# One forgetting-attention and gated-FFN kernel: gates loaded once and first, one decay product in half batch 0, first constants as tasks, a new order

## The chip, the core and the metric

The kernel runs on one core of a Trainium2 chip. A core has a matrix engine (TensorE, PE in the views, with its weight loads as PEld), a vector engine (VectorE, DVE), an activation engine (ScalarE, ACT), a general engine (GpSimd, POOL) and a queue engine that here only issues DMA (SyncE, SP). Each works through its own instructions in the order in which they were written, and waits for the others by semaphores. The metric is the time of one execution on the chip in microseconds.

## The reference

Eight batches of eight heads, 576 positions, head width 64. Attention with a decay that sums the logarithms of gates along the sequence, then a feed-forward stage 1024 wide with a short convolution as its gate. `attn_out` is the product of `attn` with V, and `hp` is `h` with one row of zeros at each end.

```python
scores = scale * np.matmul(q, k.transpose(0, 1, 3, 2))
log_f = np.log(np.clip(f, 0.0001, 1.0))
cum = np.cumsum(log_f, axis=-1)
decay = cum[:, :, :, None] - cum[:, :, None, :]
scores = np.where(causal, -1000000000.0, scores + decay)
scores = scores - np.max(scores, axis=-1, keepdims=True)
attn = np.exp(scores)
attn = attn / (np.sum(attn, axis=-1, keepdims=True) + 1e-09)
...
x = np.ascontiguousarray(attn_out.transpose(0, 2, 1, 3)).reshape(B, S, H * D)
...
h = np.maximum(x @ w_in, 0.0)
...
for k in range(K):
    conv_out += conv_w[k][None, None, :] * hp[:, k:k + S, :]
gate = 1.0 / (1.0 + np.exp(-conv_out))
return (h * gate @ w_out).astype(np.float32)
```

## The kernel before, in words

**Tiles.** The work is cut into 16 half batches of four heads (`hb` 0 to 15) for attention and 8 batches (`b`) for the feed-forward stage. A half batch holds two pairs of heads. For each pair PE makes the diagonal blocks of the score matrix (task `sd`) and, for each head, the blocks right of the diagonal (`so`); the last 64 positions of the four heads are one more task (`st`). ACT exponentiates them (`ed`, `eo`, `et`, lines 355, 372 and 334). PE multiplies by V (`pv`, lines 391 and 396), DVE normalises (`n`, `m`, lines 405 and 407), PE turns the result over (`t`, line 416), and DVE or ACT copies it (`tx`, line 419). Then for each of eight slices of the 1024 wide layer: PE `f` (line 431), ACT relu `r` (442), DVE convolution `c` and `d` (448, 450), ACT tanh or sigmoid `a` (453), DVE gate `g` (460, 458). PE makes the output from all eight slices, `o` (line 476); `e` copies it out of PSUM and `s` stores it.

**PSUM.** It is cut into four buffers of two banks, `ps`. Every PE task takes one and the task that reads it gives it back, so at most four results stand unread.

**Q, K and the decay.** Half batches 0 and 1 load Q and K plainly (`ld`), PE transposes them in nine pieces (`tp`, line 166), and ACT or DVE copies each block out of PSUM while it shifts the bits (`cl`, lines 172 and 174). From half batch 2 on, a transposing DMA brings them in (`q`, line 180), and up to 7 DVE clamps them in place (`cl`, line 186). The positions of Q and K use only every other row; rows in between carry the decay, so that one product gives scores and decay at once. They come from an image in DRAM, which the kernel writes (`ki`, line 281, three DMAs, from the tile `kc`) and reads back for each half batch (`rw`, lines 204 and 205, two DMAs). Half batch 0 doesn't wait for that: with `PAIRS = 2` all its four heads add the decay by two more matmuls after the score matmul (lines 317 and 319), one with `kc` as the stationary operand, one with the selection `sel_q`.

**The decay chain.** The gates `f` are loaded twice, into the upper and lower 64 partitions of one tile (lines 224 and 225, ACT's queue). `dca` clips (DVE, 534), `dcl` takes the logarithm (ACT, 268) and loads the table for exp (269), `dcs` sums (DVE, 272), `dck` makes `kc` (275, 276): the rounded values in partitions 0 to 63 and what rounding left, the low part, in 64 to 127. The constants (`ident`, `mask`, selections) and the first fills are written ahead of all tasks.

**The order.** No scheduler runs. `ORDER`, a string of task names, is written out by hand of a planner; `Plan.play` calls the tasks in that order, and each engine gets its instructions in that order. A name with `@` says which engine takes a task that several can do. `va` casts V (its large part `.0`, its small part `.1`), `wic` and `woc` cast the weights.

Of the kernel before, what the change touches and what calls it, by code (L numbers as in the profile page):

```python
# [700 lines left out]
```

## Time and profile before

| what | us |
|---|---|
| three timed runs | 245.17, 246.23, 246.70 |
| median | 246.23 |
| span of the profiled execution, first to last instruction | 244.7 |
| PE busy in the span | 228.6 |
| DVE busy | 205.5 |
| ACT busy | 206.8 |
| POOL busy | 51.9 |

The profiled execution's own time beyond its span is not recorded; its span lies 1.5 us below the median of the timed runs. A row of a timeline or of the chain begins with its start and its length in us; L166 is line 166; `x9` says how many instructions were put together. What stands in square brackets is idle time of the engine ahead of the row, and who ended it. ACTq and SPq are those engines' sequencers issuing DMAs. The lengths of matmuls overlap, since matmuls are pipelined, so the step from one start to the next is what one costs.

### The profile page before, as it was taken

To read this page: it belongs to the slowest core of one execution; us is meant where nothing else is said; L and a number is where in the kernel's file an instruction comes from. 1 tells how busy PE (TensorE), PEld (TensorE's weight loads), DVE (VectorE), ACT (ScalarE), POOL (GpSimd) and SP (SyncE) were. 2 spreads that over 40 slices of the span, in tenths; PEclk is the share of its full clock that TensorE was granted. 3 is DMA by queue.
4 is the path that set the end of the run, shared out by engine and by line. 5 is a ranking of instruction groups with operands and counts; after the bars stand their busy time and mean duration, and the time that the engine had idled before them with its cause. 6 is when DMAs were issued, how large, how long until landed. Compare 5 with 4: busy or idle time off the path is not lost.

```text
span 244.7 us, 6393 instructions
## 1 busy us (share of the span) xinstructions
PE 228.6 (93%) x2627; PEld 146.1 (60%) x2627; DVE 205.5 (84%) x324; ACT 206.8 (85%) x278; POOL 51.9 (21%) x77
## 2 busy tenths in 40 slices
...
GB/s 189 334 169 250 278 184 189 223 198 306 196 216 196 169 182 220 238 268 251 224 212 274 194 198 269 270 102 196 265 198 227 195 209 4 106 173 77 171 85 216
DMA packets 120424, 49.68 MB, mean 203 GB/s; under 512 B 109879, under 2 KB 110647, under 8 KB 120395
## 3 DMA queue, kind: packets, MB, share of 16 engines
...
q10 hardware_dynamic: 322, 0.47, 0.6%
q8 instruction: 20, 0.33, 0.6%
...
HBM read 21.11 MB, written 10.17 MB: 128 GB/s over the span
## 4 chain that ended last, share of the span: by engine, by line
PE 81%; DMA 5%; DVE 5%; ACT 5%; issue 1%; SPq 1%; ACTq 0%; DVEq 0%
PE ps L476 26%; PE ps L431 23%; PE ps L314 15%; PE ps L391 7%; DMA qk<-image 3%; PE ps L322 3%; PE ps L396 3%; DMA u<-in_f_dram 2%; PE ps L416 2%; ACT qk L172 2%; DVE u L450 2%; DVE u L448 1%; ACT ht L442 1%; ACT pp L372 1%; PE ps L317 1%
## 5 line engine op out<-in xcount | busy, mean ns | idle before, releaser
L431 PE MATMUL ps<-xt,w_in_f 128*128 128x512 f16 (+1 forms) x512 | 71.0, 288 | 0.4 <-DVE xt L419 0.4
L372 ACT ACTIVATE pp<-ps 128x1024 f16<-128x1024 f32 x64 | 64.8, 1032 | 3.7 <-PE ps L314 2.3
L476 PE MATMUL ps<-w_out_f,hg 128*128 128x512 f16 x288 | 66.8, 379 | 0.0
L314 PE MATMUL ps<-qk 128*128 128x128 bf16 (+2 forms) x576 | 63.9, 241 | 2.1 <-DMA qk<-image 0.9
L448 DVE SCALAR_TENSOR_TENSOR u<-ht,cwt 128x576 f32<-128x576 f16 x64 | 52.4, 832 | 4.4 <-ACT ht L442 4.2
L450 DVE SCALAR_TENSOR_TENSOR u<-ht,cwt,u 128x576 f32<-128x576 f16 x64 | 53.9, 856 | 0.5
L453 ACT ACTIVATE hg<-u,cw 128x576 f16<-128x576 f32 x64 | 48.7, 782 | 6.1 <-DVE u L450 6.0
L431 PEld LDWEIGHTS <-w_in_f 128*128 128x128 f16 x512 | 34.7, 99 | 29.4 <-issue 1.3
L314 PEld LDWEIGHTS <-qk 128*128 128x128 bf16 x576 | 39.4, 98 | 19.2 <-issue 2.5
L442 ACT ACTIVATE ht<-ps 128x576 f16<-128x576 f32 x64 | 41.0, 664 | 6.4 <-PE ps L431 2.8
L476 PEld LDWEIGHTS <-hg 128*128 128x128 f16 x288 | 26.9, 98 | 28.9
L460 DVE SCALAR_TENSOR_TENSOR hg<-hg,ht 128x576 f16<-128x576 f16 x51 | 38.6, 767 | 0.6 <-ACT hg L453 0.5
L358 POOL TENSOR_SCALAR_AFFINE_SELECT pp<-pd 128x1024 f16<-128x1024 f32 x16 | 19.7, 1244 | 53.6 <-ACT pd L355 53.6
L391 PE MATMUL ps<-va,pp 128*128 128x65 f16 x640 | 25.3, 194 | 1.7 <-DVE va L219 1.7
L391 PEld LDWEIGHTS <-pp 128*128 128x128 f16 x640 | 23.0, 98 | 4.2 <-DVE va L219 1.9
L407 DVE TENSOR_TENSOR xm<-ps,rc 128x896 f16<-128x896 f32 (+1 forms) x32 | 23.9, 751 | 0.5
L355 ACT ACTIVATE pp<-ps 128x1024 f16<-128x1024 f32 x16 | 16.6, 1038 | 5.2 <-PE ps L314 4.0
L219 POOL CAST va<-vf 128x1024 f16<-128x1024 f32 x8 | 10.0, 1247 | 34.3 <-PE ps L314 18.8
L355 ACT ACTIVATE pd<-ps 128x1024 f32<-128x1024 f32 x16 | 16.2, 1023 | 1.2 <-PE ps L314 0.5
L405 DVE RECIPROCAL rc<-ps 128x14 f32<-128x14 f32 (+1 forms) x32 | 6.6, 207 | 10.2 <-PE ps L396 4.9
L322 PE MATMUL ps<-mask,ident 128*128 128x512 bf16 (+1 forms) x40 | 14.4, 364 | 0.4 <-ACT pp L372 0.3
L481 ACT COPY ob<-ps 128x1024 f32<-128x1024 f32 (+1 forms) x14 | 12.9, 918 | 0.3 <-issue 0.2
...
## 6 DMA issues: line engine op xcount, KB each, us to landing
...
```

Source lines behind the costliest of these rows:

```text
L314: nc.tensor.matmul(o, tk[:, h * S + k0:h * S + k0 + 128], tq[:, h * S + q0:h * S + q0 + n], start=first, stop=last and not by_matmul(hb, h))
L355: nc.scalar.activation(o, ps_of(f"sd{i}").rearrange("p (s c) -> p s c", s=2), AF.Exp, scale=SCALE)
L372: nc.scalar.activation(pair(i)[:, s, 512:1536], ps_of(f"so{i}.{s}"), AF.Exp, scale=SCALE)
L391: nc.tensor.matmul(ps[:, c:c + D + 1], block(hb, h, m, n), va[:, h, m, 0:D + 1], start=(m == 0), stop=(m == n))
L407: nc.vector.tensor_tensor(xm[:, CUT * D * u:CUT * D * u + nj * k * D].rearrange("p (j x d) -> p j x d", x=k, d=D), got[:, :, :, 0:D], r.un ...
L431: nc.tensor.matmul(ps[:, t0:t1], w_in_f16[:, cc, 128 * ff:128 * (ff + 1)], xt[:, cc // 2, x:x + t1 - t0], start=(cc == 0), stop=(cc == NCC ...
L442: nc.scalar.activation(ht_of(b, ff)[:, 2:2 + S], ps_of(f"f{b}.{ff}")[:, 0:S], AF.Relu, scale=1.0 if (b, ff) in LATE else 0.5)
L448: nc.vector.scalar_tensor_tensor(u, ht[:, 1:1 + S], cwt[:, ff, 0:1], ht[:, 2:2 + S], op0=ALU.mult, op1=ALU.add)
L450: nc.vector.scalar_tensor_tensor(u, ht[:, 3:3 + S], cwt[:, ff, 1:2], u, op0=ALU.mult, op1=ALU.add)
L453: nc.scalar.activation(hg_of(b, ff), u_t[slot[f"c{b}.{ff}", "u"]], AF.Sigmoid if (b, ff) in LATE else AF.Tanh, scale=cw[:, ff, 1:2])
L460: nc.vector.scalar_tensor_tensor(hv, hv, 1.0, ht_of(b, ff)[:, 2:2 + S], op0=ALU.add, op1=ALU.mult)
L476: nc.tensor.matmul(ps[:, 512 * j:512 * (j + 1)], w, w_out_f16[:, ff, :], start=(ff == 0), stop=(ff == NFF - 1))
```

## The change: what it does

- The gates are loaded once, into 64 partitions, as the first DMA of SP (task `fl`), and no longer twice on ACT's queue. The chain `dca`, `dcl`, `dcs` works on 64 partitions. The second instruction of `dck` reads partitions 0 to 63 and writes the low part into 64 to 127. The load of the exp table is a task of its own, `dct`.
- Half batch 0 adds the decay by one matmul in place of two. Its stationary operand is `row_k[h]`, which four new DVE instructions make (`dk0` to `dk3`), each `kc` times a selection column plus a sign column; its moving operand is `row_q`, ones with eight rows of the sum (`dcq`, DVE).
- First constants become tasks: `un` (identity in fp16), `zm` and `zv` (fills on POOL). Four matmuls on the identity, 512 wide, are a new first task of PE, `wu`. The mask matmul takes the bf16 identity.
- `ORDER` is new from end to end, with other engines for some tasks. From its tags: `va` part `.0` on DVE 11 times (4 before), on POOL 2 (8), on ACT 3 (4); part `.1` on DVE 2 (4), POOL 6 (6), ACT 8 (6); `woc` on DVE 3 times (0), on POOL 1 (4); `tx` on ACT 3 times (2), DVE 8 (9); the image write `ki` on ACT (SP before); `rw` on ACT 6 times (2), SP 1 (5). Evacuations `e1.1`, `e3.2` and `e7.4` go from ACT to DVE, `e4.0` from DVE to ACT.

The diff, cut to its core, with the first two lines of the new order. The order before is one line, which begins with `dca cw ld0 ld1 ld0.0.0 tp0.0.0 dcl ld0.1.0 ld0.0.1 tp0.0.1 tp0.1.0 v0.0 ld0.1.1 ld1.0.1 ld1.0.0 dcs dck`.

```diff
+fl wu ld0 ld0.0.0 ld0.0.1 tp0.0.0 ld0.1.0 tp0.0.1 dca ld1 dcl dct un dcs dck zm cl0.0.0@ACT ld1.0.0 tp0.1.0 ld1.0.1
+cl0.0.1@ACT ki@ACT cw tp1.0.0 cwt zv tp1.0.1 dcq@DVE cl1.0.0@DVE wd dk0 ld0.1.1 cl0.1.0@ACT tp0.1.1 cl0.1.1@ACT dk1
...
-    PAIRS = 2
+    DIRECT = 1
...
-    fsb, cum = u_t[0], u_t[1]
+    fsb, cum = u_t[0][0:BH], u_t[1][0:BH]
+    row_k = [pp_t[NP - 1 - h // 4].bitcast(BF16).rearrange("p s c -> p (s c)")[:, 768 * (h % 4):768 * (h % 4) + 640]
+             for h in range(DIRECT * HH)]
+    row_q = xt_t[NXT - 1].bitcast(BF16)[:, 0, 0:S]
...
-    nc.scalar.dma_start(fsb[0:BH], f.rearrange("b h s -> (b h) s"))
-    nc.scalar.dma_start(fsb[BH:128], f.rearrange("b h s -> (b h) s"))
+    def load_gates():
+        nc.sync.dma_start(fsb, f.rearrange("b h s -> (b h) s"))
...
+    nc.vector.tensor_scalar(pick, hfx[:, 0:8], lit[:, 2:3], None, op0=ALU.is_equal)
+    nc.vector.tensor_scalar(sign, hfx[:, 32:40], lit[:, 0:1], -1.0, op0=ALU.is_equal, op1=ALU.mult)
...
-        nc.vector.tensor_scalar(kc, cum, float(-1.0 / SCALE), None, op0=ALU.mult)
-        nc.vector.scalar_tensor_tensor(kc[BH:128], cum[BH:128], float(-1.0 / SCALE), kc[BH:128],
+        nc.vector.tensor_scalar(kc[0:BH], cum, float(-1.0 / SCALE), None, op0=ALU.mult)
+        nc.vector.scalar_tensor_tensor(kc[BH:128], cum, float(-1.0 / SCALE), kc[0:BH],
                                        op0=ALU.mult, op1=ALU.subtract)
+    def decay_q(e):
+        if e == "ACT":
+            nc.scalar.activation(row_q[32:40], cum[0:8], AF.Copy, scale=float(-1.0 / SCALE))
+        else:
+            {"POOL": nc.gpsimd, "DVE": nc.vector}[e].tensor_scalar(row_q[32:40], cum[0:8], float(-1.0 / SCALE), None, op0=ALU.mult)
+    def decay_k(h):
+        nc.vector.tensor_scalar(row_k[h][:, 0:S], kc, pick[:, h:h + 1], sign[:, h:h + 1], op0=ALU.mult, op1=ALU.add)
...
+    def warm_up():
+        for x in range(4):
+            nc.tensor.matmul(ps_of("wu")[:, 512 * (x % 2):512 * (x % 2 + 1)], ident_b,
+                             ident_b.unsqueeze(1).broadcast_to((128, 4, 128)), start=True, stop=True)
...
-        if by_matmul(hb, h):
-            nc.tensor.matmul(o[0:m], kc[:, k0:k0 + m], sel_k[:, h:h + 1].broadcast_to((128, n)),
-                             start=False, stop=False)
-            nc.tensor.matmul(o, sel_q[:, h, :], kc[:, q0:q0 + n], start=False, stop=last)
+        if own:
+            nc.tensor.matmul(o, row_k[HH * hb + h][:, k0:k0 + 128], row_q[:, q0:q0 + n], start=False, stop=last)
...
+    add("dcq", "POOL/ACT/DVE", ["dcs"], decay_q)
+    for h in range(DIRECT * HH):
+        add(f"dk{h}", "DVE", ["dck"], lambda h=h: decay_k(h))
...
-                ready = [["dck"] + [f"cl0.{p}.{side}" for side in range(2)] for p in range(2)]
+                ready = [["dcq"] + [f"dk{HH * hb + 2 * p + s}" for s in range(2)] + [f"cl{hb}.{p}.{side}" for side in range(2)]
+                         for p in range(2)]
```

ACT at the start of the program, before: the two gate loads, the logarithm and the table (L268, L269), three copies of turned Q and K (L172), then the first exponentials (L355, L372), with a copy between them.

```order
L224 DMA u_120<-in_f_dram 64x576
L225 DMA u_120<-in_f_dram 64x576
L226 ACT_TABLE_LOAD
L227 DMA pd_105<-in_moe_conv_w_dram 3x1024
L268 ACTIVATE u_120<-u_120 128x576
L269 ACT_TABLE_LOAD
L172 ACTIVATE qk_85<-ps_130,lim 128x1152
L172 ACTIVATE qk_85<-ps_131,lim 128x1152
L172 ACTIVATE qk_85<-ps_132,lim 128x1152
L355 ACTIVATE pp_95<-ps_131 128x2x512
L372 ACTIVATE pp_95<-ps_132 128x1024
```

And ACT at the same place now (L330 is the logarithm, L227 are the copies, L421 the first exponential; the convolution weights, L282, stand ahead of this piece).

```order
L283 ACT_TABLE_LOAD
L330 ACTIVATE u_119<-u_119 64x576
L605 ACT_TABLE_LOAD
L227 ACTIVATE qk_84<-ps_129,lim 128x1152
L227 ACTIVATE qk_84<-ps_130,lim 128x1152
L351 DMA image<-kc 64x576 x3
L227 ACTIVATE qk_84<-ps_131,lim 128x1152
L227 ACTIVATE qk_84<-ps_130,lim 128x1152
L227 ACTIVATE qk_85<-ps_128,lim 128x1152
L259 DMA qk_85<-image 1x2304
L260 DMA qk_85<-image 2x2304
L421 ACTIVATE pp_94<-ps_130 128x2x512
```

The three image writes and the read of the image for half batch 1 (`rw1`, L259 and L260) moved from SP to ACT, and stand ahead of the first exponential; all five copies that ACT makes stand ahead of it too.

DVE behind the convolution ratios (`cwt`), before: copies of turned Q and K (L174), the clamps of half batch 2 (L186), the first normalisation (L405).

```order
L306 TENSOR_TENSOR cwt<-cw,cwt 128x8
L174 TENSOR_SCALAR qk_85<-ps_130,lim 128x1152
L174 TENSOR_SCALAR qk_86<-ps_130,lim 128x1152
L221 CAST va_92<-vf_89 64x4x64
L174 TENSOR_SCALAR qk_86<-ps_131,lim 128x1152
L186 TENSOR_SCALAR qk_87<-qk_87,lim 128x2304 x2
L405 RECIPROCAL rc_110<-ps_130 128x14
```

And now (L344 is `dcq`, L229 the copies, L347 the four `dk`, L241 the clamps).

```order
L377 TENSOR_TENSOR cwt<-cw,cwt 128x8
L344 TENSOR_SCALAR xt_113<-u_120 8x576
L229 TENSOR_SCALAR qk_85<-ps_130,lim 128x1152
L347 TENSOR_SCALAR pp_99<-kc,pick,sign 128x576 x3
L229 TENSOR_SCALAR qk_85<-ps_129,lim 128x1152
L229 TENSOR_SCALAR qk_85<-ps_131,lim 128x1152
L347 TENSOR_SCALAR pp_99<-kc,pick,sign 128x576
L241 TENSOR_SCALAR qk_86<-qk_86,lim 128x2304 x2
```

Five instructions for the decay operands came in among the copies, three of them (L347 x3) ahead of two copies that half batch 1 needs; all three copies now belong to half batch 1.

SP at its start, before: Q and K of half batch 0 (L159) with a V load (L211) between, half batch 1, the rest of V, the image (L281), the transposing loads (L180).

```order
L159 DMA hg<-in_q_dram 128x576 x2
L159 DMA hg<-in_k_dram 128x576
L211 DMA vf_89<-in_v_dram 128x8x64
L159 DMA hg<-in_k_dram 128x576
L159 DMA hg<-in_k_dram 128x2x576
L159 DMA hg<-in_q_dram 128x2x576
L211 DMA vf_89<-in_v_dram 128x8x64 x3
L211 DMA vf_89<-in_v_dram 64x8x64
L281 DMA image<-kc 64x576 x3
L180 DMA_TRANSPOSE qk_87<-in_k_dram 128x2304
```

And now (L280 is the gates, L214 Q and K, L266 V, L584 a weight piece, L235 the transposing loads).

```order
L280 DMA u_119<-in_f_dram 64x576
L214 DMA hg<-in_q_dram 128x576
L214 DMA hg<-in_k_dram 128x576
L214 DMA hg<-in_q_dram 128x576
L214 DMA hg<-in_q_dram 128x2x576
L214 DMA hg<-in_k_dram 128x2x576
L214 DMA hg<-in_k_dram 128x576
L266 DMA vf_88<-in_v_dram 128x8x64
L584 DMA ob_124<-in_moe_w_in_dram 128x2x512
L235 DMA_TRANSPOSE qk_86<-in_k_dram 128x2304
```

The gates stand first, half batch 1 stands ahead of the last piece of half batch 0, and most of V and the image stand no longer ahead of the transposing loads.

More of the change, by code (lines that the diff above doesn't have):

```diff
@@ new lines @@
+fl wu ld0 ld0.0.0 ld0.0.1 tp0.0.0 ld0.1.0 tp0.0.1 dca ld1 dcl dct un dcs dck zm cl0.0.0@ACT ld1.0.0 tp0.1.0 ld1.0.1
+cl0.0.1@ACT ki@ACT cw tp1.0.0 cwt zv tp1.0.1 dcq@DVE cl1.0.0@DVE wd dk0 ld0.1.1 cl0.1.0@ACT tp0.1.1 cl0.1.1@ACT dk1
+v0.0 tp1.1.0 dk3 tp1.1.1 wi2 cl1.1.0@ACT q2.1 cl1.0.1@DVE cl1.1.1@DVE dk2 sd0 rw1@ACT q2.0 v0.3 so0.0 ed0 sd1 so1.1
+st0 ed1 eo1.1 so0.1 et0 eo0.0 v0.2 so1.0 sd2 sd3 cl2.0 eo0.1 eo1.0 v0.4 so2.0 cl2.1 so3.1 ed2 v0.1 va0.0@POOL ed3
+so3.0 va0.1@ACT wi3 pv0.0 wic2@POOL n0.0 va1.0@DVE eo2.0 wi0 eo3.1 eo3.0 v1.0 m0.0 st1 so2.1 et1 pv0.1 rw2@SP n0.1
@@ new lines @@
+eo2.1 pv1.0 wi1 m0.1 sd4 n1.0 m1.0 q3.0 st2 va1.1@POOL et2 pv1.1 q3.1 t0 ed4 n1.1 wic1@POOL m1.1 t1 so4.1 tx0@DVE sd5
+tx1@ACT q4.1 wic0@POOL wic3@POOL ed5 f0.0 r0.0 f0.1 eo4.1 so5.0 r0.1 cl3.0 v1.2 f0.2 r0.2 f0.3 c0.0 f0.4 d0.0 h0 a0.0
+cl3.1 rw3@ACT so4.0 r0.4 v1.1 r0.3 c0.1 c0.2 v1.3 q4.0 f0.5 so5.1 wo2 v1.4 g0.0 d0.2 c0.4 eo5.0 d0.4 eo4.0 d0.1 a0.4
+r0.5 cl4.1 f0.6 sd6 eo5.1 va3.0@DVE ed6 sd7 a0.2 so6.1 c0.3 q5.1 ed7 eo6.1 q5.0 va2.0@DVE g0.4 g0.2 f0.7 r0.6 d0.3
+cl4.0 q6.0 r0.7 rw4@ACT c0.5 va2.1@ACT st3 et3 so7.1 so6.0 pv2.0 c0.7 n2.0 a0.3 va3.1@POOL eo6.0 d0.5 so7.0 d0.7 m2.0
@@ new lines @@
+eo7.1 eo7.0 woc2@DVE pv2.1 pv3.0 q7.0 pv3.1 wo0 v2.0 a0.7 n2.1 cl5.1 v2.1 a0.5 a0.1 wo1 m2.1 n3.0 cl5.0 t2 n3.1 sd9
+m3.0 m3.1 tx2@ACT t3 g0.1 tx3@DVE g0.5 so9.0 rw5@ACT g0.7 ed9 wo3 f1.0 sd8 eo9.0 c0.6 so8.0 f1.1 g0.3 r1.0 c1.0 ed8
+d0.6 eo8.0 cl7.0 f1.2 st4 r1.1 d1.0 so9.1 r1.2 h1 v2.3 v2.2 sd10 et4 woc0@DVE eo9.1 f1.3 so8.1 a0.6 a1.0 eo8.1 r1.3
+f1.4 c1.2 g0.6 d1.2 woc1@DVE c1.1 sd11 r1.4 so11.1 c1.3 ed10 f1.5 g1.0 eo11.1 cl6.0 woc3@POOL d1.1 q6.1 a1.2 ed11
+so10.1 v2.4 o0.0 eo10.1 st5 va5.0@DVE va4.0@ACT et5 d1.3 g1.2 o0.1 cl6.1 c1.4 r1.5 f1.6 a1.3 e0.0@ACT q7.1 pv4.0
@@ L19 @@
+o7.1.1 o7.3.3 o7.4.5 o7.0.3 g7.7 o7.4.6 o7.4.7 e7.4@DVE o7.2.5 o7.3.4 o7.2.6 o7.3.5 o7.2.7 o7.3.6 s5.1 o7.3.7 o7.0.4
+s7.4@SP o7.0.5 e7.2@ACT o7.0.6 o7.0.7 o7.1.2 e7.3@DVE s7.2@ACT o7.1.3 s7.3@ACT o7.1.4 e7.0@DVE o7.1.5 s7.0@SP o7.1.6
+o7.1.7 e7.1.1@ACT e7.1.0@DVE s7.1.1@SP s7.1.0@SP
 """
@@ L263, with pads, levels @@
-    for t in range(NVA):
-        nc.gpsimd.memset(va_t[t][:, :, :, D:VW], 1.0)
-        nc.gpsimd.memset(va_t[t][64:128, :, NKB - 1, 0:D], 0.0)
+    def pads():
+        for t in range(NVA):
+            nc.gpsimd.memset(va_t[t][:, :, :, D:VW], 1.0)
+            nc.gpsimd.memset(va_t[t][64:128, :, NKB - 1, 0:D], 0.0)
+    def levels():
+        nc.gpsimd.memset(plus, 1.0)
+        nc.gpsimd.memset(minus, -1.0)
+        nc.gpsimd.memset(zero, 0.0)
+        for t in range(NHT):
+            nc.gpsimd.memset(ht_t[t][:, 1:2], 0.0)
+            nc.gpsimd.memset(ht_t[t][:, S + 2:S + 3], 0.0)
@@ L287, in constants @@
         nc.sync.dma_start(blank, zero[0:60])
-    def warm_up(name):
-        for x in range(2):
-            nc.tensor.matmul(ps_of(name)[:, 512 * x:512 * (x + 1)], quiet[:, 0:128], quiet, start=True, stop=True)
+    def warm_up():
+        for x in range(4):
+            nc.tensor.matmul(ps_of("wu")[:, 512 * (x % 2):512 * (x % 2 + 1)], ident_b,
+                             ident_b.unsqueeze(1).broadcast_to((128, 4, 128)), start=True, stop=True)
     def conv_weights():
```

119 lines of the change are left out of this document (72 added, 47 removed).

## The prediction

> **What bounds the kernel now.** I read first the view of each engine's busy time in chosen stretches, because a share over the whole program hides the start. Its columns are the stretch, its length, the busy time of PE, PEld, DVE, ACT and POOL (with instructions), the granted clock, the busy share of the DMA engines, and GB/s.
>
> ```profile
> span 244.7 us, 6393 instructions
> ...
> 8.00:40.00 32.00, 29.93 (x409) 23.80 (x409) 16.88 (x29) 23.99 (x25) 6.52 (x7) 1.00 1.06 232
> 40.00:60.00 20.00, 17.21 (x235) 11.48 (x233) 18.65 (x28) 17.98 (x26) 2.75 (x3) 0.91 1.07 239
> 60.00:80.00 20.00, 20.00 (x189) 11.83 (x184) 19.33 (x27) 19.94 (x29) 5.01 (x4) 1.00 1.09 204
> 80.00:230.00 150.00, 149.99 (x1761) 93.47 (x1758) 139.72 (x211) 138.33 (x192) 32.27 (x33) 1.00 0.89 199
> 230.00:240.60 10.60, 10.60 (x50) 4.64 (x48) 6.80 (x12) 4.62 (x7) 0.00 (x0) 1.00 0.29 104
> ```
>
> From 60 us to 240.6 PE is busy for 180.59 of 180.6 us at full clock. What it loses lies ahead of that: 2.07 us idle in 8 to 40, 2.79 in 40 to 60, and a clock of 0.91 in that stretch, 0.09 x 20 = 1.8 us more. Lengths of matmuls overlap, so a full stretch can hide small gaps, but a new order behind 60 us has little to win. The time falls by what the start gets shorter, as long as the other engines keep up. The chain of waits (start, length, what) shows what sets the start and the end:
>
> ```profile
> 1.44 5.62 DMA u<-in_f_dram
> 7.16 0.47 DVE u L534
> 7.66 0.68 ACT u L268
> 8.36 1.28 ACT L269
> 9.65 2.52 ACT qk L172 x2
> 12.22 0.58 PE ps L322
> ...
> 14.74 0.19 PE ps L317
> ...
> 25.15 7.33 DMA qk<-image
> ...
> 224.66 3.92 PE ps L431 x32
> 228.58 12.10 PE ps L476 x56
> ```
>
> The second copy of the gates lands at 1.44 + 5.62 = 7.06; clip, logarithm, exp table and two copies of turned Q and K follow in one piece, and the first scores begin at 12.22. From then ACT's exponentials set the pace. The end is PE's output products and one copy behind them, and the change leaves that as it is.
>
> **The gates.** One copy in place of two, issued first. When did the first copy land? In SP's list the first K load waited for it (engine, what for, total, times, longest), and went out at 4.60:
>
> ```profile
> SPq L159 <- DMA u<-in_f_dram: 0.7, 1, 0.7
> 4.60 0.38 SPq L159 DMA_DIRECT2D hg<-in_k_dram  x1
> ```
>
> I take 4.5 for the landing, with 4.0 (a queue ahead of the others) and 7.06 (no gain) as ends: 2.5 us earlier. The chain behind it on DVE, and what else DVE has to do there:
>
> ```profile
> 8.37 1.36 DVE L272 TENSOR_TENSOR_SCAN u<-one,u 128x576 f32<-128x576 f32 x1 [0.75 <-ACT u L268]
> 9.76 0.46 DVE L275 TENSOR_SCALAR kc<-u 128x576 bf16<-128x576 f32 x1
> 10.26 0.76 DVE L276 SCALAR_TENSOR_TENSOR kc<-u,kc 64x576 bf16<-64x576 f32 x1
> 11.04 0.18 DVE L299 COPY cw<-ps 128x24 f32<-128x24 f32 x1
> 12.21 0.16 DVE L306 TENSOR_TENSOR cwt<-cw,cwt 128x8 f32<-128x8 f32 x1
> 12.29 1.47 DVE L174 TENSOR_SCALAR qk<-ps,lim 128x1152 uint16<-128x1152 uint16 x1
> ```
>
> Half as many partitions carry the same 576 columns, so I leave the durations alone: the low part takes 0.76 for 64 partitions already. From 4.6: 0.47 + 0.68 + 1.36 + 0.46 + 0.76 plus small steps is 3.7, so `kc` is ready at 8.3 (11.02 before), the logarithm at 5.7 and the exp table at 7.0 (9.64 before). ACT then copies `cl0.0.0` and `cl0.0.1` (1.26 each, half of the 2.52 above) to 9.5.
>
> **What stands ahead of the first exponential now.** ACT's own list, and the issue of the image on SP (SPq, ACTq: issuing):
>
> ```profile
> 13.48 1.82 SPq L281 DMA_DIRECT2D image<-kc  x3
> ...
> 14.50 1.02 ACT L355 ACTIVATE pp<-ps 128x1024 f16<-128x1024 f32 x1 [1.14 <-PE ps L319]
> 24.88 0.38 ACT L334 ACTIVATE pt<-ps 128x256 f16<-128x256 f32 x1 [0.33 <-PE ps L319]
> 30.74 1.94 ACT L372 ACTIVATE pp<-ps 128x1024 f16<-128x1024 f32 x2
> ...
> 52.70 0.23 ACTq L204 DMA_DIRECT2D qk<-image  x1
> 52.83 1.04 ACT L372 ACTIVATE pp<-ps 128x1024 f16<-128x1024 f32 x1
> 52.97 0.66 ACTq L205 DMA_DIRECT2D qk<-image  x1
> ```
>
> Before, the exponentials of half batch 0 ran from 14.50 to 25.26, broken by waits and two copies of half batch 1, and those of half batch 1 ended at 30.74 + 1.94 = 32.68.
>
> Now DVE: `cwt` from 9.3 (its matmuls stand behind turned Q and K) takes 12.37 - 11.04 = 1.33, to 10.7; `dcq` 0.3, to 11.0; `cl1.0.0` 1.47, to 12.5; `dk0`, `dk1`, `dk3`; then `cl1.0.1` and `cl1.1.1`, 2.94. For `dk` no row stands: I take 0.46, L275's price, the same output; the lower end is 0.16, the price of the smallest operation (12.21), the upper 0.76. So the copies end at 12.5 + 1.4 + 2.9 = 16.8 (15.9 to 17.7). ACT: `ki`, whose issue of 1.82 overlaps work (at 52.70 to 53.63 ACT issued two DMAs and executed L372 meanwhile), then `cl0.1.0`, `cl0.1.1`, `cl1.1.0`, to 15.8; then `rw1`, which waits for the copies on DVE (16.8) and for the image to land, and issues for 0.23 + 0.66. Behind it in ACT's order wait all exponentials. The first starts at 17.7, which is 3.2 later than before.
>
> But then nothing breaks them: no copies, and all scores of half batch 0 wait ready in PSUM. Six of 0.92 (pitch inside 30.74's pair, rounded down as two overlap) and one of 0.38 make 6.0, so half batch 0 ends at 23.7 (25.26 before), and half batch 1, with the same 6.0 and a small cast, at 30.3 (32.68 before): 2.4 us gained. With the gates at 4.0 and the cheaper `dk` it is 3.7. I take 3.0, near the middle of the two. With the landing at 7.06 nothing of the 2.4 is left.
>
> **One product fewer.** 16 diagonal products 128 wide at 0.19 x 128/448 = 0.054, four each of 448, 320, 192 and 64 wide, 4 x 0.19 x 1024/448 = 1.7, and four small tails: about 2.7 us of PE time. ACT's six exponentials of 0.92 cover it: PE's work for the same six groups is, without the second product, shorter than they are. So it isn't added. Where that cover is missing, in the first group at least, it is a share of the 2.7, and I leave it to the range.
>
> **Warm-up and clock.** Four matmuls 512 wide cost 4 x 12.10/56 = 0.86 at full clock, 1.7 at half, before any Q or K is there: nothing. Whether PE is then fast is read here:
>
> ```profile
> 8.06 4.07 PE L166 MATMUL ps<-ident_b,hg 128*128 128x128 bf16 x36
> ...
> 49.99 1.62 PE L391 MATMUL ps<-va,pp 128*128 128x65 f16 x32 [1.67 <-DVE va L219]
> 52.25 1.94 PE L431 MATMUL ps<-xt,w_in_f 128*128 128x512 f16 x8
> ```
>
> Eight of L431 take 1.94 at 52.25, and 8/32 x 3.92 = 0.98 late in the program: half clock, behind a gap of 1.67 ahead of `pv2.0`. In the start the 36 turnings took 0.113 each at the granted rate then. The Trainium skill, "TensorE: Matmul & The Clock Gate", Part 1, asks some 3.4 us of sustained work for the full rate and about as long an idle window for falling back; Part 4 says that PE-mode transposes don't count as work there. The trace agrees with neither in full: the gap before 49.99 was 1.67 long and the rate was half behind it. By the rule on transposes the scores of half batch 0 would begin cold; rival C has that case.
>
> **SP.** Most of V (four pieces) now goes out behind the two transposing loads of half batch 2, and `ki` and most of `rw` leave SP.
>
> ```profile
> 18.50 2.40 SPq L180 DMA_TRANSPOSE qk<-in_q_dram  x1
> ```
>
> Two such issues put V back by 4.8, so it goes out at some 13 and lands, at 7.33 like the slowest read above, by some 20. The cast of V is wanted when half batch 0's last exponential ends, at 23.7, so it costs nothing, with under 3 us in hand.
>
> **Casts from POOL to DVE.** Ten large casts (seven `va.0`, three `woc`) go to DVE, two small `va.1` and one `tx` leave it, and one evacuation more comes.
>
> ```profile
> 49.25 0.68 DVE L219 CAST va<-vf 128x1024 f16<-128x1024 f32 x1
> 54.98 0.81 DVE L450 SCALAR_TENSOR_TENSOR u<-ht,cwt,u 128x576 f32<-128x576 f16 x1
> 56.89 1.31 POOL L526 CAST w_out_f<-ob 128x1024 f16<-128x1024 f32 x1 [12.46 <-DMA ob<-in_moe_w_out_dram]
> 57.34 1.48 DVE L450 SCALAR_TENSOR_TENSOR u<-ht,cwt,u 128x576 f32<-128x576 f16 x1
> L481 DVE COPY ob<-ps 128x1024 f32<-128x1024 f32 x3 | 3.7, 1219 | 2.0 <-ACT xt L419 1.9
> ```
>
> A cast costs DVE 0.68. But beside a cast on POOL a DVE operation took 1.48 in place of 0.81, so each cast that leaves POOL gives up to 0.67 back: 10 x (0.68 - 0.67), near nothing. If nothing comes back, DVE has 9 x 0.68 (one lies ahead of 40 us) - 0.5 - 0.76 + 1.22 = 6.1 us more behind 40 us. I take nothing and price the other end as rival S. ACT gets the image and four more `rw` at 0.9 of issue each, and has 190 - 17.98 - 19.94 - 138.33 = 13.75 us idle between 40 and 230.
>
> **The rivals.**
> F, the forecast: 244.7 - 3.0 = 241.7 for the profiled span; the median of the runs lies 1.5 above the span, so 243.2; its own range is 241.5 to 244.5, and its chance 0.40.
> G, more is gained: the gap of 1.67 before `pv2.0` goes and with it the half clock, 1.8. Both hang on V's cast on DVE, which now stands elsewhere. 246.2 - 3.0 - 3.4 = 239.8. Against it: the first FFN slices still share DVE with the casts. 0.16.
> H, the gates change nothing at the end: the image, written and read back, decides. `qk<-image` took 7.33 at 25.15 behind weight loads; if the write or a read lands 2.5 later than I count, ACT stands in order behind `rw1` and the gain is gone: 246.2. A single load that lands no earlier than 7.06 comes to the same. 0.18. The skill, "DMA: Bandwidth & Descriptors", "Issuing engines are not separate DMA queues", says that another issuing engine saves only issue time; by it moving `ki` and `rw` to ACT wins nothing at the DMA engines.
> C, cold scores: PE runs the first scores at half clock, since only turnings and idle time lie between the warm-up and them. The stretch at half clock near 50 lies inside 49.99 to 54.19; if this one is 3.2 long it costs half of that, 1.6: 244.8. Against it: ACT, not PE, sets that stage's pace. 0.08.
> S, slower: DVE becomes the bound. It was busy 18.65 + 19.33 + 139.72 = 177.70 of 190 us from 40 to 230, 0.935. With 6.1 more it is 183.8. At the share of before that takes 196.6, 6.6 more; less the 3.0, 3.6 slower: 249.8. It decides from a share of 183.8/193 = 0.952 on: if DVE can't be filled above that, the gain is gone. For it: DVE feeds PE in a fixed order and waits for relu. Against it: it reached 19.33/20 = 0.967 in 60 to 80. 0.18.
>
> **How the numbers follow.** About 1% is what a measurement of this kernel can tell from no change: faster is below 243.8, slower above 248.7. Below: all of G and 0.30 of F's 0.40, 0.46. Above: 0.16 of S's 0.18. The rest, 0.38, is between. The range leaves out G's better half beyond 238.8 and the larger part of S: 238.8 to 248.7.
>
> **What would show it.** Right: the clip begins by 5.0, `kc` ends near 8.3, the first exponential begins near 17.7 and none has a copy between, half batch 1's last ends near 30.3, no half clock near 50. The decay products: one matmul behind each score matmul. Wrong: the first exponential beyond 19, ACT waiting ahead of the first read of the image, PE idle behind 60 us with DVE as its releaser, a DVE share above 0.96 there with more than 150 us for the old 80 to 230.

## The result, and the profile after

| kernel | median of four | runs | span of the profiled execution |
|---|---|---|---|
| before | 245.74 | 245.17 to 246.70 | 244.7 |
| changed | 249.34 | 247.64 to 251.45 | 247.5 |

The changed kernel takes 1.0121 times as long as the one before, with a 95% interval of 1.008 to 1.0162. Here and below the medians and ranges are of all runs, while the ratios leave out slow ones, more than 1.5% above the fastest of the same kernel, as the 251.45 here. The forecast was 243.2. Line numbers below belong to each kernel's own listing; a line that an experiment shares with the changed kernel can stand some numbers further down.

The view of busy time by stretches, as in the prediction (stretch, length, then PE, PEld, DVE, ACT, POOL busy, granted clock, DMA share, GB/s), of the changed kernel:

```profile
span 247.5 us, 6316 instructions
...
8.00:40.00 32.00, 28.99 (x373) 22.18 (x371) 16.72 (x31) 22.85 (x27) 5.36 (x6) 1.00 1.20 237
40.00:60.00 20.00, 16.08 (x232) 10.81 (x229) 19.68 (x32) 18.35 (x26) 2.06 (x1) 1.00 1.11 202
60.00:80.00 20.00, 19.65 (x192) 11.87 (x191) 20.00 (x29) 19.15 (x26) 1.73 (x2) 1.00 1.14 237
80.00:100.00 20.00, 16.89 (x215) 11.21 (x213) 15.74 (x25) 14.32 (x20) 2.11 (x3) 1.00 1.07 206
100.00:230.00 130.00, 129.98 (x1501) 80.14 (x1498) 123.00 (x186) 120.01 (x168) 27.59 (x25) 1.00 0.83 189
230.00:243.40 13.40, 13.40 (x69) 6.05 (x66) 10.42 (x17) 6.86 (x10) 0.00 (x0) 1.00 0.41 147
```

One stretch of the kernel before, for the place that matters:

```profile
80.00:100.00 20.00, 19.99 (x304) 14.19 (x302) 18.80 (x31) 18.52 (x27) 1.38 (x2) 1.00 1.01 200
```

From 40 us to the end the changed kernel's PE is busy 16.08 + 19.65 + 16.89 + 129.98 + 13.40 = 196.00, the old one's 17.21 + 20.00 + 149.99 + 10.60 = 197.80. So at 40 us the new start is ahead by 1.8, less what the half clock near 50 (0.91 in that stretch) added to the old one's busy time. PE's idle time behind 40 us is 3.92 + 0.35 + 3.11 + 0.02 = 7.40, against 2.80 before. That is 4.6 more, and 4.6 - 1.8 = 2.8 is the difference of the spans. Of the 4.6, 3.1 lie between 80 and 100, where the old kernel lost nothing; ACT and DVE stand still there as well.

ACT between 80 and 92 (start, length, what; in brackets the idle time ahead of the row and who ended it), with SP's transfers and PE's gaps in the same stretch, all of the changed kernel:

```profile
80.31 0.22 ACTq L259 DMA_DIRECT2D qk<-image  x1
82.21 0.56 ACTq L260 DMA_DIRECT2D qk<-image  x1
82.82 1.02 ACT L438 ACTIVATE pp<-ps 128x1024 f16<-128x1024 f32 x1 [2.92 <-DVE xm L473]
89.52 0.21 ACTq L259 DMA_DIRECT2D qk<-image  x1
90.42 1.94 ACT L421 ACTIVATE pp<-ps 128x1024 f16<-128x1024 f32 x2 [2.86 <-DMA qk<-image]
...
77.85 0.59 SPq L355 DMA_DIRECT2D image<-pd  x1
79.14 0.61 SPq L357 DMA_DIRECT2D blank<-zero  x1
82.36 3.65 SPq L266 DMA_DIRECT2D vf<-in_v_dram  x4
...
86.42 0.38 PE L388 MATMUL ps<-mask,ident_b 128*128 128x512 bf16 x1 [0.93 <-ACT ht L508]
91.50 0.66 PE L482 MATMUL ps<-ident,xm 128*128 128x128 f16 x9 [1.72 <-ACT pp L421]
```

These are `rw6` and `rw7`, the reads of the decay image for half batches 6 and 7. Each stands in ACT's order ahead of exponentials, and those wait until it is issued. The row of 82.82 names DVE's normalisation (L473), but that is only what happened to end near there: at 82.21 the second half of the read went out, and the exponential began 0.05 behind its issue. What the reads wait for can be read from the program as built, where the waits of each instruction stand:

```
L259 DMA qk_86<-image 1x2304 [waits DMAHW1_49,DMAHW0_49]
L260 DMA qk_86<-image 2x2304 [waits DMAHW3_49,DVE_49]
L259 DMA qk_87<-image 1x2304 [waits DMAHW7_49]
L260 DMA qk_87<-image 2x2304 [waits DMAHW1_49,DVE_49]
```

Every DMA of this program signals its end on one of eight counters, which are given out in turn along the program's list of instructions. A DMA waits, before it is issued, for the one that had the same counter eight DMAs ahead, on whatever queue that is. For `rw6` those are two of the writes that `zc` makes (counter 1: L355, issued at 77.85; counter 3: L357, issued at 79.14), for `rw7` a V load (counter 7, the third of the four from 82.36). None of these has anything to do with the data that is read. The other waits in the list were over by then: counter 0 is the read of half batch 2 into the same tile, the clamps on DVE ended at 77.74 and 83.34, and counter 1 of `rw7` is `rw6` itself. On SP such a wait holds only later transfers; on ACT it holds the exponentials.

### The profile page after: what moved, and what is told of

Read it like the earlier page. It is cut to its first block, busy times and chain, and to the rows that moved or that the text cites. A ratio compares the mean times of both kernels' runs of the same rounds, so it can differ in the third digit from the quotient of the medians.

```text
span 247.5 us, 6316 instructions
## 1 busy us (share of the span) xinstructions
PE 229.7 (93%) x2595; PEld 145.1 (59%) x2595; DVE 212.2 (86%) x337; ACT 206.1 (83%) x278; POOL 45.1 (18%) x73
## 4 chain that ended last, share of the span: by engine, by line
PE 67%; DVE 15%; ACT 11%; DMA 2%; issue 2%; SPq 0%; ACTq 0%; DVEq 0%
PE ps L542 22%; PE ps L497 18%; PE ps L382 12%; PE ps L457 7%; ACT pp L438 5%; DVE u L516 4%; DVE u L514 3%; ACT pp L421 3%; PE ps L462 2%; PE ps L221 2%; DVE hg L526 2%; DVE xm L473 2%; PE ps L482 2%; DMA hg<-in_k_dram 2%; ACT hg L519 2%
## 5 line engine op out<-in xcount | busy, mean ns | idle before, releaser
L497 PE MATMUL ps<-xt,w_in_f 128*128 128x512 f16 (+1 forms) x512 | 70.0, 286 | 0.7 <-ACT pp L421 0.3
L382 PE MATMUL ps<-qk 128*128 128x64 bf16 (+2 forms) x576 | 62.1, 240 | 1.3 <-ACT pp L438 1.1
L514 DVE SCALAR_TENSOR_TENSOR u<-ht,cwt 128x576 f32<-128x576 f16 x64 | 54.0, 856 | 4.6 <-ACT ht L508 4.4
L516 DVE SCALAR_TENSOR_TENSOR u<-ht,cwt,u 128x576 f32<-128x576 f16 x64 | 52.1, 831 | 0.6
L526 DVE SCALAR_TENSOR_TENSOR hg<-hg,ht 128x576 f16<-128x576 f16 x51 | 37.9, 767 | 1.3 <-ACT hg L519 0.9
L424 POOL TENSOR_SCALAR_AFFINE_SELECT pp<-pd 128x1024 f16<-128x1024 f32 x16 | 20.3, 1276 | 57.5 <-ACT pd L421 57.3
L457 PE MATMUL ps<-va,pp 128*128 128x65 f16 x640 | 24.8, 193 | 2.0 <-ACT pp L438 1.3
L457 PEld LDWEIGHTS <-pp 128*128 128x128 f16 x640 | 22.5, 97 | 4.3 <-issue 1.9
L473 DVE TENSOR_TENSOR xm<-ps,rc 128x896 f16<-128x896 f32 (+1 forms) x32 | 23.8, 752 | 0.5
L421 ACT ACTIVATE pp<-ps 128x1024 f16<-128x1024 f32 x16 | 16.4, 1045 | 5.5 <-DMA qk<-image 2.9
L388 PE MATMUL ps<-mask,ident_b 128*128 128x512 bf16 (+1 forms) x40 | 14.5, 364 | 2.5 <-ACT ht L508 1.6
L421 ACT ACTIVATE pd<-ps 128x1024 f32<-128x1024 f32 x16 | 16.1, 1021 | 0.1
L241 DVE TENSOR_SCALAR qk<-qk,lim 128x2304 uint16<-128x2304 uint16 x12 | 10.3, 864 | 2.8 <-DMA qk<-in_q_dram 2.8
```

Of the source, the lines that this page charges most:

```text
L382: nc.tensor.matmul(o, tk[:, h * S + k0:h * S + k0 + 128], tq[:, h * S + q0:h * S + q0 + n], start=first, stop=last and not own)
L421: nc.scalar.activation(o, ps_of(f"sd{i}").rearrange("p (s c) -> p s c", s=2), AF.Exp, scale=SCALE)
L457: nc.tensor.matmul(ps[:, c:c + D + 1], block(hb, h, m, n), va[:, h, m, 0:D + 1], start=(m == 0), stop=(m == n))
L473: nc.vector.tensor_tensor(xm[:, CUT * D * u:CUT * D * u + nj * k * D].rearrange("p (j x d) -> p j x d", x=k, d=D), got[:, :, :, 0:D], r.un ...
L497: nc.tensor.matmul(ps[:, t0:t1], w_in_f16[:, cc, 128 * ff:128 * (ff + 1)], xt[:, cc // 2, x:x + t1 - t0], start=(cc == 0), stop=(cc == NCC ...
L514: nc.vector.scalar_tensor_tensor(u, ht[:, 1:1 + S], cwt[:, ff, 0:1], ht[:, 2:2 + S], op0=ALU.mult, op1=ALU.add)
```

## The experiments

Theory W is this wait. Theory D is the rival of the prediction with the price on the slow side, that the casts now on DVE make it the bound. A third question is where the start's gain went. The expectations number the runs in the order in which they were written down: the first is "The two reads back on SP", the third "All new parts, in the old order", the fourth "The reads of the new order put into the kernel before", the seventh `rw1` earlier with the new parts. The kernel before was run again with each group. Its medians were 246.01 with the two reads, the casts, the reads put into the kernel before and all new parts; 246.21 with the writes behind the reads, both runs of `rw1` earlier and `rw1` on SP; 246.27 with the three without weight loads; 245.57 with the last two.

**The two reads back on SP.**

```diff
-rw6@ACT
+rw6@SP
...
-rw7@ACT
+rw7@SP
```

> The changed kernel, with the reads of the decay image for half batches 6 and 7 (rw6, rw7) issued by SP in place of ACT; everything else, the order too, is as changed. Theory W (ACT stands still while the issue of these two reads waits for other transfers, and its exponentials behind it come late): the two idle stretches of ACT before 82.82 and 90.42 (2.92 and 2.86 us) go, PE's busy time in 80 to 100 rises from 16.9 to over 19, and the time falls by 2 to 3 us, to 246.3 to 247.3. Theory D (the casts that moved to DVE make DVE the bound): the time stays at 249.3 within 0.7.

Measured: 247.44 (246.86 to 247.67), 1.0055 of before (1.0033 to 1.0078).

```profile
80.00:100.00 20.00, 19.75 (x263) 13.15 (x262) 19.45 (x29) 17.61 (x25) 1.47 (x2) 1.00 0.99 183
```

PE's busy time between 80 and 100 is back at 19.75, and of the 3.6 us between the two medians (249.34 and 245.74) 1.9 are gone. W holds for that part. D alone could not bring it, since no cast moved.

The stretch from 80 to 100 won 2.86, more than the 1.9, because this run's start was later, though nothing there had changed:

```profile
13.71 2.52 ACT L234 ACTIVATE qk<-ps,lim 128x1152 uint16<-128x1152 uint16 x2 [0.66 <-PE ps L228]
19.32 0.23 ACTq L266 DMA_DIRECT2D qk<-image  x1
19.67 0.65 ACTq L267 DMA_DIRECT2D qk<-image  x1
20.36 1.94 ACT L428 ACTIVATE pp<-ps 128x1024 f16<-128x1024 f32 x2 [4.14 <-PE ps L392]
...
31.16 1.07 ACT L445 ACTIVATE pp<-ps 128x1024 f16<-128x1024 f32 x1
```

ACT stood for 4.14 us, and the first exponential came at 20.36 (18.49 in the changed kernel). The copies that `rw1` needs had ended at 16.23 on ACT and 16.71 on DVE, but its first half went out at 19.32. By the program as built it also waits for the first image write, issued at 7.02, and, by its counter, for the transposing K load of half batch 2, whose issue kept SP from 8.77 to 14.85. So W is there at `rw1` too, and its size differs from run to run.

**The casts back on the engines of before.**

```diff
-va1.0@DVE va3.0@DVE va5.0@DVE va10.0@DVE va11.0@DVE va13.0@DVE woc0@DVE woc1@DVE woc2@DVE
+va1.0@POOL va3.0@ACT va5.0@POOL va10.0@POOL va11.0@POOL va13.0@POOL woc0@POOL woc1@POOL woc2@POOL
...
```

> The changed kernel, with every cast of V and of the output weights on the engine that had it before (20 tags changed; seven large V casts and three weight casts leave DVE for POOL or ACT again); the order is as changed. Theory D: DVE is relieved of some 6 us, and the time falls by 2 to 4 us, to 245.3 to 247.3. Theory W: the two idle stretches of ACT between 79.9 and 90.4 stay, PE has no other idle time behind 100, and the time stays at 249.3 within 0.7.

Measured: 251.66 (250.24 to 252.41), 1.0222 (1.0177 to 1.0267), slower than the changed kernel by 2.3. D falls: relieving DVE of casts costs time here. DVE's busy time over the span did not fall (213.7, against 212.2 in the changed kernel), though ten large casts had left it. Beside casts on POOL five of its operations between 50 and 75 took 1.59 to 1.92, where the same alone take 0.74 to 0.87. Here is one of the five, with the cast beside it and the next DVE operation behind it:

```profile
70.06 1.06 POOL L599 CAST w_out_f<-ob 128x1024 f16<-128x1024 f32 x1 [0.45 <-DMA ob<-in_moe_w_out_dram]
...
70.14 1.59 DVE L248 TENSOR_SCALAR qk<-qk,lim 128x2304 uint16<-128x2304 uint16 x1
71.66 0.80 DVE L523 SCALAR_TENSOR_TENSOR u<-ht,cwt,u 128x576 f32<-128x576 f16 x1
```

In the changed kernel such a clamp took 0.87. Two of the ten casts went to ACT (busy 206.9, against 206.1); what that costs is not parted from this. My expectation for W missed as well: the idle stretches of ACT at `rw6` and `rw7` are gone in this run. ACT gets to `rw6` some 3 us later (83.64 in place of 80.31), so the write has landed by then. The time had been lost ahead of it: between 40 and 80 PE is idle for 7.29 us, against 4.28 in the changed kernel.

**The reads of the new order put into the kernel before.**

```diff
-rw6@SP
+zc
+rw6@ACT
...
-zc
...
-rw7@SP
+rw7@ACT
```

> The kernel before, with two things of the new order put in: rw6 and rw7 are issued by ACT, and the writes of the constants into the image (zc) stand ahead of rw6. Theory W: ACT stands still ahead of these reads as in the changed kernel, PE is idle for 1 to 3 us between 75 and 100 where it was idle for none, and the time is 246.7 to 248.7. Theory D: no cast has moved, 245.7 within 0.7.

Measured: 253.45 (251.42 to 254.75), 1.0294 (1.0226 to 1.0363), 7.4 us slower, far more than I expected. ACT's and PE's rows in this run:

```profile
85.13 0.22 ACTq L262 DMA_DIRECT2D qk<-image  x1
85.80 0.55 ACTq L263 DMA_DIRECT2D qk<-image  x1
86.40 1.94 ACT L430 ACTIVATE pp<-ps 128x1024 f16<-128x1024 f32 x2 [6.44 <-DMA image<-pd]
...
87.47 1.54 PE L489 MATMUL ps<-xt,w_in_f 128*128 128x512 f16 x8 [4.61 <-ACT pp L430]
```

Here the releaser is named: `image<-pd`, a write of `zc`, which is the DMA eight places ahead of the second half of `rw6` (L263). Most of the 6.44 was over by then: the first half (L262) went out at 85.13, and what stands eight places ahead of that is a V load, issued at about 79.65. The clamps that it also waits for had ended at 80.14. W holds in kind; its price depends on how long before those transfers were issued, and on what the gap does to PE: behind the 4.61 its granted clock was 0.81 from 85 to 90 and 0.85 from 90 to 95 (1.00 there in the kernel before), which is 0.34 x 5 = 1.7 us more.

**The same, with the writes behind the reads.**

```diff
-zc
 rw6@ACT
...
 rw7@ACT
+zc
```

> The fourth experiment (the kernel before, rw6 and rw7 on ACT) with one change: the writes of the constants into the image stand behind rw7 and not ahead of rw6. The transfers eight places ahead of rw6 are then two V loads, not a V load and the image write. Theory W: ACT's wait of 6.4 us falls below 3, and the one look is at 246 to 250. Rival (an image read on ACT at this place holds it whatever stands ahead): the wait stays at 5 to 7, 252 to 255.

Measured in one run: 252.74. The wait did not fall below 3:

```profile
85.36 1.94 ACT L430 ACTIVATE pp<-ps 128x1024 f16<-128x1024 f32 x2 [6.92 <-DMA vf<-in_v_dram]
```

The size I expected was wrong, and by the numbers written down beforehand the rival won. The name of the releaser moved, though: now it is a V load, and V loads are what stands eight places ahead of both halves of the read in this order. So removing the writes only put another recent transfer in their place.

**All new parts, in the old order.**

```diff
+fl wu wd
 dca
+un
...
 dcl
+dct
...
 dck
+dcq@DVE dk0 dk1
...
 cwt
+dk2 dk3
...
```

> The new parts (one load of the gates, first on SP; the low part across partitions; one decay product in half batch 0; first constants as tasks; the warm-up) with the order and the engines of before, into which the new tasks are set at the places of their first use. My theory of the start (the decay chain is 2 to 2.5 us shorter, five small DVE operations cost about 1.2 of it): the first exponential starts near 13.3 in place of 14.50, half batch 1 ends near 31.5, and the time is 243.8 to 245.2, 0.5 to 2 below the kernel before. Rival (the start's gain is spent in waits between 30 and 60, as in the changed kernel): 245.7 within 0.7.

Measured: 245.90 (244.57 to 248.56), 0.999 (0.9959 to 1.0021): no difference, the rival's number. The start itself is faster than I thought, and what eats it shows in four rows (first and second row ACT, then PE, then SP):

```profile
12.08 1.02 ACT L428 ACTIVATE pp<-ps 128x1024 f16<-128x1024 f32 x1 [0.85 <-PE ps L392]
26.69 1.02 ACT L428 ACTIVATE pp<-ps 128x1024 f16<-128x1024 f32 x1 [5.92 <-PE ps L389]
...
25.19 0.61 PE L389 MATMUL ps<-qk 128*128 128x128 bf16 x4 [3.94 <-DMA qk<-image]
...
21.38 0.71 SPq L267 DMA_DIRECT2D qk<-image  x1
```

The first exponential starts at 12.08 (14.50 before), and half batch 0 ends at 20.8 (25.26 before). Then ACT waits 5.92 us, because `rw1`, the image read of half batch 1, went out at 21.38 behind two transposing loads and a weight piece. Half batch 1 starts at 26.69; before it started at 26.75. So the parts of the change are worth 4.5 us at half batch 0, and nothing at half batch 1. In the changed kernel with its own order the first exponential comes at 18.49: the order gives up 6.4 us of what the parts won there, to have the copies of half batch 1 done first.

**`rw1` earlier on SP: with the new parts, and in the kernel before.**

```diff
-q2.0
...
-wi1 wic1@POOL
...
 rw1@SP
+q2.0 wi1
...
-wi2
+wic1@POOL
 wic0@POOL
-wi3
...
+n0.0 m0.0
 cl2.0 cl2.1 rw2@SP
-n0.0 m0.0
+wi2 wi3
```

> The third experiment (the new parts in the old order) with SP's order changed at the start: rw1 ahead of the second transposing load of half batch 2 and of the first weight load; rw2 ahead of two weight loads. Theory I (in the third experiment half batch 0 was done at 20.8, and half batch 1 stood until its image read landed, so the start's gain was lost in this queue): half batch 1 starts at 22.5 to 24 in place of 26.69, and the time is 242.5 to 244.5. Rival: behind it the weights or half batch 2's loads are late, 245.9 within 0.7.

> The kernel before with that order of SP's first loads alone, none of the new parts. Theory I: half batch 0 ends at 25.26 as before, ACT's idle time of 1.49 behind it goes, and no more than that can be won: 244.4 to 245.9. If it wins as much as the run with the new parts, those parts bring nothing.

Measured: with the new parts 247.53 (245.66 to 249.66), 1.0039 (0.9997 to 1.0081); the kernel before 252.93, 1.0267 (1.0193 to 1.0341). Both forecasts of the time missed. With the new parts half batch 1 started when I expected, at 22.93, but PE then waited further on:

```profile
29.88 0.38 PE L389 MATMUL ps<-qk 128*128 128x128 bf16 x4 [2.03 <-DMA qk<-image]
44.87 0.38 PE L389 MATMUL ps<-qk 128*128 128x128 bf16 x4 [1.43 <-DMA qk<-image]
```

Its runs also differ in PE's mean granted clock, from 1.0 (245.66 and 245.72 us) to 0.986 (248.91 and 248.92). In the kernel before half batch 1 did not start earlier at all, since there the copies were late and not SP. It lost 6.7 us. DVE stood for 2.27 and 1.36 us (at 41.14 and 43.38) for transposing loads that now go out later, where the kernel before stood for none, and PE later for 1.90 (at 47.69, for ACT) and 1.42 (at 49.48, for an image read); how the whole 6.7 comes about was not followed up.

**Three weight loads left out** (with the new parts and `rw1` early; in the kernel before; and in the changed kernel with the two reads on SP). Three of the four pieces of the first weights are not loaded; their casts read the piece that is (`j == 2` in the third of these kernels).

```diff
-        nc.sync.dma_start(ob, src)
+        if w == "wo" or j == 1:
+            nc.sync.dma_start(ob, src)
```

> The seventh experiment (new parts, old order, rw1 early) with three of the four 512 KB loads of the first weights left out; their casts read the one piece that is loaded, so that all other work stays (the output is then not the reference's, and 1.5 MB less is moved in the first 35 us). Theory L (from 10 to 60 us the DMA engines are full, share over 1 in every stretch, and what the start wins is spent waiting for loads behind weights): the waits for image reads at 29.88 and 44.87 (2.03 and 1.43) shrink, and the time falls from 247.5 by 2 to 4 us, to 243.5 to 245.5. Rival (what is behind, DVE and ACT from 40 on, sets the pace): 247.5 within 1.

> The kernel before with the same three loads left out in the same way. Theory L: the wait of 0.86 for the image read at 32.52 goes, and since the compute chain of the start is the late one there, little more is won: 244.7 to 245.9, more than half a microsecond above the run with the new parts. Rival: 246.1 within 0.7 and no difference between the two.

> The changed kernel with rw6 and rw7 on SP, with the same three loads left out. Theory L: 247.4 falls by 1 to 3 us, to 244.5 to 246.5, as rw1, V and rw2 land earlier. Rival: 247.4 within 0.7.

Measured: 242.14 (241.21 to 243.05), 0.9837 (0.9777 to 0.9896), 246.68, 1.0014 (0.9984 to 1.0044), and 249.01 (245.83 to 250.51), 1.0061 (1.0012 to 1.0109). The first is lower still than theory L said: without those loads the end is 4.1 us ahead of the kernel before, nearly the 4.5 of the start. Its wait of 2.03 is 0.71, and 60 to 80 is full again:

```profile
28.45 0.38 PE L389 MATMUL ps<-qk 128*128 128x128 bf16 x4 [0.71 <-DMA qk<-image]
...
60.00:80.00 20.00, 20.00 (x179) 11.50 (x178) 19.32 (x27) 19.11 (x27) 3.14 (x2) 1.00 1.10 215
```

The second lies above the 244.7 to 245.9 that I expected. That is the use of the pair: the loads cost the old start nothing, and the new one 5.4 us by the medians. Against the two runs with early `rw1` at clock 1.0 (245.66 and 245.72) it is 3.5, so a part of the 5.4 goes with the lower clock of the others. For the changed kernel L is left open. By the median it missed. But its two runs at a clock of 0.999 and 1.0 took 246.27 and 245.83, within L's range and 1.0 to 1.6 below the two of the first experiment at that clock (247.28 and 247.44); the other eight, at 0.976 to 0.993, took 248.16 to 250.51, and what lowers the clock in them was not found. Its start, with a first exponential at 19.20, is not held by a load alone:

```profile
13.84 3.04 PE L228 MATMUL ps<-ident_b,hg 128*128 128x128 bf16 x27 [1.45 <-DVE qk L236]
```

There PE turns Q and K of half batch 1 ahead of any score and waits for a free PSUM buffer, until DVE has copied one.

**`rw1` on SP in the changed order.**

```diff
-rw1@ACT
+rw1@SP
```

> The changed kernel with rw6 and rw7 on SP as in the first experiment, and rw1, the read of half batch 1, on SP too. Theory W (a read on ACT stands until the transfer eight places ahead of it in the program has landed, for rw1 the transposing load of half batch 2): the first exponential starts at 16.3 to 17.5 in place of 18.49, half batch 1 ends at 29.5 to 31, and the time falls by another 0.5 to 2 us against the first experiment, to 245.4 to 246.9. Rival: what the start wins is spent in the waits between 40 and 80: 247.4 within 0.7.

Measured, with `rw6` and `rw7` on SP too: 248.21 (246.78 to 249.14), 1.0073 (1.0043 to 1.0103). The forecast missed. The first exponential came at 19.16, released by PE's scores, and V came late behind the read, as PE's waits show (who, for whom, total, times, longest):

```profile
PE ps L464 <- POOL va L281: 1.8, 1, 1.8
```

So putting `rw1` on SP does not make the changed start earlier. That it costs nothing on ACT is not shown by this: in the first experiment's profile ACT stood behind it.

**Weight pieces kept, but later.**

```diff
-wi2 wi3
...
-wic2@POOL
...
 q3.1
+wi2 wi3
...
+wic2@POOL
 wic3@POOL
```

> The seventh experiment with every load kept, and two of the four first weight pieces (those that are needed from the fifth slice on) moved behind the transposing loads of half batch 3, their casts with them. Theory P (it is the place of the loads): the waits of PE for image reads at 29.88 and 44.87 shrink as without these loads, 243 to 245. Theory B (it is the bytes: the DMA engines are full from 10 to 70, so what is moved back is waited for there): 246 to 248.

In the second of the two `wi0` also moves behind `rw2`.

> As the run before it, and a third weight piece behind the image read of half batch 2. Theory P: 242.5 to 244.5, or the cast of that piece comes late for the first slices (f0.0 near 34 to 35) and it is no better than the run before. Theory B: 246 to 248.

Measured: 246.36 (245.63 to 249.58), 1.0026 (0.9999 to 1.0053), and 249.25 (248.98 to 251.54), 1.017 (1.0124 to 1.0216). Neither comes near 242. In the first the waits for image reads did shrink, as theory P said (PE's went from 3.7 us in all to 0.9), but the time did not: DVE now stood for a transposing K load that goes out later, and ACT and PE stood behind it.

```profile
42.15 0.88 DVE L248 TENSOR_SCALAR qk<-qk,lim 128x2304 uint16<-128x2304 uint16 x1 [3.83 <-DMA qk<-in_k_dram]
...
45.28 0.58 PE L389 MATMUL ps<-qk 128*128 128x128 bf16 x4 [3.15 <-DVE u L523]
```

In the second that wait of DVE is 5.11. So theory B is nearer, in its mechanism too, though the second is slower than either allowed. No version with all loads beats the kernel before.

## Why the prediction was wrong

**The step that failed** is in the part on the casts, its last sentence: that ACT "gets the image and four more `rw` at 0.9 of issue each", to be paid from 13.75 us of idle time. I priced the moved reads by their issue, and looked at what each waits for only in the first, `rw1`, and there not at its counter. Two of them, `rw6` and `rw7`, made ACT stand for 2.92 and 2.86 us in place of 0.9, and PE for 3.1 between 80 and 100. Taking them back brought 1.9 of the 6.1 us between the forecast and the median; the rest is mostly the second error, below. The rows of before could not show this wait as it is, but they held its kin: `rw2` took 7.33 to land, and SP's issues waited for other transfers in the row of the first K load. Rival H had the mechanism (ACT stands in order behind `rw1`), with a gain lost as its worst end. It came true in the first experiment's profile, where what `rw1` waited for was a transposing load.

**"A new order behind 60 us has little to win"** was right, and stood for half of the matter: a stage in which PE has no idle time can only lose. I gave that no price.

**The start was told well, but its gain did not hold.** In the changed kernel's profile the clip started at 3.74 (4.5 forecast for the landing), `kc` was done at 8.42 (8.3), the first exponential came at 18.49 (17.7):

```profile
3.57 1.12 POOL L324 MEMSET zero<- 64x1152 bf16 x1
3.74 1.26 DVE L603 TENSOR_SCALAR u<-u 64x576 f32<-64x576 f32 x1
7.67 0.75 DVE L337 SCALAR_TENSOR_TENSOR kc<-u,kc 64x576 bf16<-64x576 f32 x1
9.64 1.94 ACTq L351 DMA_DIRECT2D image<-kc  x2
11.63 1.31 ACT L227 ACTIVATE qk<-ps,lim 128x1152 uint16<-128x1152 uint16 x1 [2.09 <-DVE xt L344]
12.87 1.10 DVE L347 TENSOR_SCALAR pp<-kc,pick,sign 128x576 bf16<-128x576 bf16 x3
16.16 1.48 DVE L229 TENSOR_SCALAR qk<-ps,lim 128x1152 uint16<-128x1152 uint16 x1 [0.80 <-PE ps L221]
18.49 1.02 ACT L421 ACTIVATE pp<-ps 128x1024 f16<-128x1024 f32 x1 [1.81 <-DVE pp L347]
29.84 1.07 ACT L438 ACTIVATE pp<-ps 128x1024 f16<-128x1024 f32 x1
```

The clip took 1.26 and not 0.47, beside a fill on POOL; `dk` took 0.37 each (0.46). Two steps on the way were wrong. Three copies of 1.26 from 9.5 on end at 13.3, not at 15.8. And the issue of `ki` overlapped only in its first write: ACT stood for 2.09 us ahead of its next copy while the other two went out. What that cost is not shown; `rw1` then waited for DVE's last copy, at 16.16 + 1.48 = 17.64. Half batch 1's last exponential ends at 30.91 (30.3 forecast, 32.68 before), so 1.8 of the 2.4 were won in this run. In the first experiment's, with the same start, it ends at 32.23, and 0.45 is won.

That 3.0 us of this carry to the end was the second error. With the two reads back on SP the time was still 1.4 above before, and the parts alone, with 4.5 at half batch 0, brought 0 in the old order. There the runs without weight loads show what took it; for the changed order it stays open. I had the view that warns of it, a DMA share of 1.06 and 1.07 from 8 to 60, and did not use it as a bound.

**Rival S** had the right sign and the wrong cause. DVE's share from 40 to 230 is (19.68 + 20.00 + 15.74 + 123.00)/190 = 0.939, almost the 0.935 of before, and the casts on DVE are a help: taking them away cost 2.3. My "near nothing" for the casts was wrong in size in the other direction, at least in this order.

**G** came true in its condition and not in its gain: there is no half clock near 50 (1.00 in 40 to 60), but the gap of 1.67 became several smaller ones, and PE's idle time there rose from 2.79 to 3.92. Nor was the 1.8 for the half clock there to be won: of the 67 runs of the kernel before that belong to the experiments, the 31 with a mean granted clock of 0.998 or more have a median of 245.90 us, the 25 with 0.994 or less one of 245.93.

**C and the warm-up.** The four matmuls changed nothing that a row shows. Nine turnings right behind them, and the first scores:

```profile
4.76 1.14 PE L221 MATMUL ps<-ident_b,hg 128*128 128x128 bf16 x9 [0.68 <-DMA hg<-in_q_dram]
...
15.84 0.63 PE L388 MATMUL ps<-mask,ident_b 128*128 128x512 bf16 x1
...
16.48 0.30 PE L382 MATMUL ps<-qk 128*128 128x128 bf16 x1
16.59 0.25 PE L385 MATMUL ps<-xt,pp 128*128 128x128 bf16 x1
16.67 0.22 PE L382 MATMUL ps<-qk 128*128 128x128 bf16 x1
16.73 0.22 PE L385 MATMUL ps<-xt,pp 128*128 128x128 bf16 x1
```

The turnings' pitch is about 0.11, and the first products' too (16.48 to 16.59), until it falls to 0.06 from 16.67 on. The scores did begin slow, but for 0.8 us behind the first matmul at 15.84, and ACT was busy then; C's 1.6 was too much. The Trainium skill, "TensorE: Matmul & The Clock Gate", Part 4, says that PE-mode transposes don't count as work for the clock, and the slow turnings here agree with it; its 3.4 us of sustained work (Part 1) are more than the 0.8 seen, unless the turnings ahead counted.

**What stays open:** of the 3.6 us between the medians 1.9 are tied to the two reads by taking them back. The other 1.4 to 1.7 go with PE gaps of 0.2 to 1.0 between 40 and 80, 4.18 in all in that run (2.79 before), that no single edit removed. Whether a place for the weight loads exists that keeps the start's gain was not found; the last two runs show two places that don't.
